# Sums of w1's gradient laid out as they are stored, and a first product with w2 begun earlier, on one Trainium2 core

## The chip, the core and the metric

The kernel runs on one core of one Trainium2 chip. Such a core has an engine for matrix products (TensorE, "PE" in the profile; its weight loads are listed apart as "PEld"), three others that compute (VectorE "DVE", ScalarE "ACT", GpSimd "POOL"), an engine that mostly issues transfers (SyncE "SP"), and 16 DMA engines that carry the transfers of all of them. Products land in PSUM, a small memory of eight banks, and are copied from there to SBUF by ACT or DVE. The metric is the device time of one execution in microseconds (us); lower is better.

## What is computed

The reference runs two kinds of layers, each twice, and differentiates the result with respect to all inputs but one. What is left out here are the set-up, and the convolution `_A_ref` in full.

```python
def _fwd_reference(A_q, A_k, A_v, A_shift_k, A_ssm_k, A_ssm_D, B_x, B_w1, B_w2):
    def _A_ref(q, k, v, shift_k, ssm_k, ssm_D):
        ...
        return q * y
    def _B_ref(x, w1, w2):
        h = jnp.einsum("bsd,df->bsf", x, w1)
        h = _silu(h)
        out = jnp.einsum("bsf,fd->bsd", h, w2)
        return out
    x = A_q
    x = x + _A_ref(_layernorm(x, axis=-1), A_k, A_v, A_shift_k, A_ssm_k, A_ssm_D)
    x = x + _B_ref(_layernorm(x, axis=-1), B_w1, B_w2)
    x = x + _A_ref(_layernorm(x, axis=-1), A_k, A_v, A_shift_k, A_ssm_k, A_ssm_D)
    x = x + _B_ref(_layernorm(x, axis=-1), B_w1, B_w2)
    return x

def reference(...):
    ...
    _out, _vjp = jax.vjp(_f, A_q, A_k, A_v, A_shift_k, A_ssm_k, A_ssm_D, B_w1, B_w2)
    _grads = _vjp(grad_out)
```

There are 2048 tokens, D = 448 channels and F = 1792 hidden features, all in bfloat16. Two results matter below. The gradient of w1 (448 x 1792) is, for each of the two dense layers, the layer's normalised input, transposed, times the gradient at the hidden features; the two layers' parts are added. The gradient at the hidden features begins with the product of the incoming gradient with w2 transposed; for the second dense layer the incoming gradient is `grad_out` itself, so this product needs nothing of the forward pass.

## The kernel before

**Opening.** `_ssm_prefix` computes the convolution once (both layers share its kernel and its k and v) by transforms written as matrix products. Its last loop is the one that matters: `_fft_stage2` makes 14 chunks of a spectrum and hands each to `cons_prod` (L461), which copies it out of PSUM, multiplies it on DVE with the two kernel spectra (`pab`, L471), stores it, and, two chunks behind, issues the inverse transform `_fft_inv_stage2_chunk` (L235, L236), whose result is copied to `B1`. PSUM is one ring of four buffers here (tag "A"). Behind the loop the first four token tiles of `grad_out` (`k.gb0`, "chunk 0") are transposed on PE (L487) and copied by DVE into `k.gT0`, a part of the tile `X` that is not in use yet (L488); the last products (`ps_y`, L496) give `Ysb`.

**Main part.** `Main.run` goes over the tokens in four chunks of 512. The generators `H` (product with w1, then silu and, beside it, a copy for the slope), `O` (product with w2), `G` (the incoming gradient times w2 transposed), `N` (its result times w1 transposed, and the layer norm's backward) and `T`/`T2` (transposes) each yield after a piece of PE's work. A string of letters fixes the order in which they take turns on PE, whose instruction order is written out by hand. `_products` (L504) makes the seven pairs of feature blocks of `H` and `G`; as 448 = 3 x 128 + 64, it puts the 64-row remainders of two blocks beside each other in two half-height tiles of the array. In the table below "G20" is `G` for the second dense layer of chunk 0, "G21" that of chunk 1:

| Where | Order before (L816, L828 to L831, L858) |
|---|---|
| in front of the first `H` | G20: two pairs, three transposes, G20: one pair |
| after the first forward layer | G20: four pairs; then G21: three pairs between transposes |
| chunk 1's stage | O G G O G G O T O T, the four G being G21's last pairs |

`G` copies each pair from PSUM into `ghT` (tag "T", five buffers, seven feature blocks each).

**Weight gradients.** Both weight gradients need all tokens, so the hidden features and their gradients are transposed by DMA and stored per feature block (`store`, L560). `Jobs` then sums them block by block, as filler: other code calls `jobs.run(n)`, and each step is four products. `load` brings a block of 2048 tokens x 128 features (`dstat`, 512 KB); `mms` (L992) has the block as the stationary side and the 448 channels as the moving side, 16 token tiles for each layer, so that the sum in PSUM is 128 features x 448 channels (L995). For w2 that is how the result is stored. For w1 it is the other way round: `fin_w1` (L1102) copies the sum to SBUF, and `flush` (L1108), one job later, turns it with four PE transposes (L1117), copies it again and stores it. Layer 2 has the moving side `n3m`, layer 1 `n1m`. The order of jobs is in `steps` (L1037): w2's blocks 0 to 6, w1's 14 blocks, w2's blocks 7 to 13. PSUM here is two banks "po", one "jb", one "tr" for the jobs and two double banks "mm" for the suffix.

**Suffix.** `_ssm_suffix` does the convolution's backward with products of its own (`ps_tr`, `ps_gkv`, `ps_gK`, and `ps_sk`, which uses tiles 32 columns wide, L1318), and calls `jobs.run` between them; `jobs.run(1000)` at its end issues what is left. POOL's queue carries most of the suffix's loads and the stores of w1's and w2's gradients.

Of the kernel before, what the change touches and what calls it, by code (L numbers as in the profile page):

```python
# [10 lines left out]
FP32 = mybir.dt.float32  # L11
BF16 = mybir.dt.bfloat16
# [285 lines left out]
def _ssm_prefix(k):  # L298
# [4 lines left out]
    with ExitStack() as es:  # L303
# [133 lines left out]
                    next(ln0, None)  # L437
        for _ in ln0:
            pass
        for i in range(7):  # L440
            _swap_halves_dma(k, KB, Ka, 2048 * i, 2048 * (i + 1), nc.gpsimd)
        stage1_kv(*prev)
# [15 lines left out]
            turn(A1f, Zkv, g)  # L458
        hold = []

        def cons_prod(ci, ps):  # L461
            sl = slice(ci * 1024, (ci + 1) * 1024)
            xs = Zf[:, sl]
            _copy(nc, bal.pick(1024), xs, ps[:])
            if ci % 2 == 1:
                st = nc.gpsimd.dma_start(out=k.SPEC_d["KV"][:, (ci - 1) * 1024:(ci + 1) * 1024], in_=Zf[:, (ci - 1) * 1024:(ci + 1) * 1024])
            if ci == 3:
                with tc.issue_after(st.ins):
                    nc.gpsimd.memset(k.w2T[0:64, 3, 0:2 * P], 0.0)
            pab = work.tile([P, 2, 1024], BF16, name="pab", tag="pab", bufs=3)  # L470
            nc.vector.tensor_tensor(out=pab[:], in0=xs.rearrange("p (a c) -> p a c", a=1).to_broadcast([P, 2, 1024]), in1=ZK[:, :, sl], op=ALU.mult)  # L471
            bal.add("dve", 1.22)
            hold.append((pab[:, 0], pab[:, 1], ci))
            if len(hold) > 2:
                pa, pb, cj = hold.pop(0)
                _fft_inv_stage2_chunk(k, pa, pb, False, B1, cj, psum)

        _fft_stage2(k, Zkv, psum, cons_prod)

        k.X = k.wk.tile([P, NT, D], BF16, name="X", tag="WX")  # L480
        k.gT0 = k.X[:].rearrange("p t d -> p (t d)")[:, 11 * D:11 * D + 2048].rearrange("p (b t) -> p b t", b=ND)
        for pa, pb, cj in hold:
            _fft_inv_stage2_chunk(k, pa, pb, False, B1, cj, psum, halves=cj == NCI - 1)
        pt = psum.tile([P, ND, 512], BF16, name="ps_t", tag="A", bufs=4)
        for b, (lo, hi) in enumerate(BLK):
            for tl in range(4):
                nc.tensor.transpose(pt[:, b, tl * P:(tl + 1) * P], k.gb0[:, tl, lo:hi], k.ident[:])  # L487
        nc.vector.tensor_copy(k.gT0, pt[:])  # L488

        B1v = B1.rearrange("p a (c n s) -> p a c n s", c=2, n=16)  # L490
        for i in range(8):
            py = psum.tile([P, 2, 512], FP32, name="ps_y", tag="A", bufs=4)
# [45 lines left out]
class Main:  # L538
# [162 lines left out]
                nc.gpsimd.dma_start(out=_pm(k.outs[0][0])[:, t - 1:t + 1, :], in_=X[:, t - 1:t + 1, :])  # L701
            yield

    def G(self, gT, res, dT=None, dv=()):
        nc, k = self.nc, self.k
        half = lambda h: self.t([P, NF // 2, 512], f"ghT{h}", "T", 5)
        res[:] = [half(0)]
        gh = res
        for fp, ps in _products(nc, lambda: self.banks("ps_g"), self.w2T, gT):
            if fp == 3:  # L710
                res.append(half(1))
            for lo, hi in self.parts(fp):
                hh, o = divmod(2 * fp + lo, 7)
                g = gh[hh][:, o:o + hi - lo, :]
                d = None if dT is None else self.dpart(dT, 2 * fp + lo, 2 * fp + hi)
                if dT is not None and fp in dv:
                    nc.vector.tensor_tensor(out=g, in0=d, in1=ps(lo, hi), op=ALU.mult)
                    continue
                if dT is None and fp in dv:
                    with self.tc.issue_after(k.ln_last.ins):  # L720
                        nc.vector.tensor_copy(g, ps(lo, hi))
                else:
                    nc.scalar.copy(g, ps(lo, hi))  # L723
                if dT is not None:
                    self.g_last = nc.vector.tensor_tensor(out=g, in0=d, in1=g, op=ALU.mult)
            yield
# [57 lines left out]
    def run(self, es):  # L784
# [22 lines left out]
            nc.gpsimd.dma_start(out=_pm(k.Y_d[:]), in_=k.Ysb[:])  # L807
        nT = self.nT()
        gh2 = []
        g20 = self.G(k.gT0, gh2, dv=(2,))  # L810

        def steps(pattern, **gens):
            for ch in pattern:
                next(gens[ch], None)

        steps("GGtttG", G=g20, t=self.T2(self.n0[0][1], nT))  # L816
        gb = gb_load(0)
        weave("H" * 7, H=self.H(0, 0, nT, r, range(14)))
        aT, dT1 = r
# [5 lines left out]

        gh21 = []
        g21 = self.G(gT, gh21)
        steps("GGGG", G=g20)  # L828
        next(g20, None)
        nT = self.nT()  # L830
        steps("tGtGtGt", G=g21, t=self.T2(self.n1[1], nT))  # L831
        r = []
# [4 lines left out]
        for c in range(4):  # L837
# [38 lines left out]
            if c < 3:  # L876
                r = []
                if c == 0:
                    weave("NTNTNHNNHHNNHHNHH", N=n, T=self.T(self.n0[1][1], nT), H=self.H(c + 1, 0, nT, r, (10, 11)))
                else:  # L880
                    weave("NHNNHHNNHHNNHHN", N=n, H=self.H(c + 1, 0, nT, r))
                gb = gb_load(c + 1)
                aT, dT1 = r
                weave("OOOOOOTOTO", O=self.O(c + 1, 0, aT), T=tg)
                self.fwd1(c + 1, [self.chain] * 4)
                g = self.G(gT, gh1, dT0)
                if c:
                    gT = self.nT()
                    self.load_gT(c + 1, gT)
                    weave("G" * 7, G=g)  # L890
                else:
                    weave("G" * 7, G=g)
                self.slope(dT1, self.last_copy)
            else:
                weave("NJNJNJNJNJNJNJN", N=n, J=jg)
                for hh in range(2):
                    self.store(("g", 1), gh2[hh], c, hh)
                weave("J" * 11 + "TJJTJJJJ", T=tg, J=jg)
                weave("GGGJJGGJJGGJJ", G=self.G(gT, gh1, dT0, (1, 3, 5)), J=jg)
# [23 lines left out]
class Jobs:  # L923


    def __init__(self, k, main):
        self.k, self.nc, self.main = k, k.nc, main
        self.pool = main.ch
        self.n_ld = self.n_bank = 0
        self.pend = None  # L930
        self.last_ld = None

    def gen(self):
# [71 lines left out]
    def group(self, fts, keys, movs, fin, tags=None):  # L1005
        ps = {}
        tags = tags or [None] * len(fts)
        for i, ft in enumerate(fts):
            st = self.load(keys[0], ft)
            ps[ft] = self.bank(tags[i])  # L1010
            yield from self.mms(ps[ft], st, movs[0](), 0, NT, True, False)
        if fts == (12, 13):
            self.go2()
        for ft in fts:
            st = self.load(keys[1], ft)
            if fts == (5, 6) and ft == 5:
                self.load_n3()
            yield from self.mms(ps[ft], st, movs[1](), 0, NT, False, True)
            fin(ft, ps[ft])
# [17 lines left out]
    def steps(self):  # L1037
        g2 = lambda: self.k.mov2
        go = lambda: self.go
        keys = (("a", 1), ("a", 0))  # L1040
        yield from self.opening()
        yield from self.group((3,), keys, (go, g2), self.fin_w2, tags=("jb",))
        yield from self.group((4,), keys, (go, g2), self.fin_w2, tags=("tr",))
        yield from self.group((5, 6), keys, (go, g2), self.fin_w2)
        wkeys = (("g", 1), ("g", 0))
        movs = (lambda: self.n3, self.n1)
        for f in range(12):
            yield from self.group((f,), wkeys, movs, self.fin_w1)
        yield from self.group((12, 13), wkeys, movs, self.fin_w1)
        for f in range(7, 13):  # L1050
            yield from self.group((f,), keys[::-1], (g2, self.go2), self.fin_w2)
        yield from self.last_block(keys[::-1], (g2, self.go2))

    def last_block(self, keys, movs):
# [5 lines left out]
        for lo, hi in ((0, 320), (320, D)):  # L1060
# [6 lines left out]
                        yield 1  # L1067
            nc.scalar.copy(o[:, lo:hi], ps[:, lo:hi])
            nc.sync.dma_start(out=k.outs[8][ft * P:(ft + 1) * P, lo:hi], in_=o[:, lo:hi])
        self.flush()  # L1070

    def go2(self):
        k = self.k
# [21 lines left out]
    def fin_w2(self, ft, ps):  # L1095
        nc, k = self.nc, self.k
        o = self.out()
        nc.scalar.copy(o[:], ps[:, :D])
        self.flush()
        (nc.gpsimd if ft < NF - 2 else nc.sync).dma_start(out=k.outs[8][ft * P:(ft + 1) * P, :], in_=o[:])  # L1100

    def fin_w1(self, ft, ps):  # L1102
        o = self.out()
        self.nc.scalar.copy(o[:], ps[:, :D])
        self.flush()
        self.pend = (ft, o)

    def flush(self):  # L1108
        nc, k = self.nc, self.k
        if self.pend is None:  # L1110
            return
        ft, o = self.pend
        self.pend = None
        out7v = k.outs[7].rearrange("(c p) f -> p c f", p=DC)
        pt = k.psum.tile([DC, ND, P], BF16, name="ps_dt", tag="tr", bufs=1)
        for dc in range(ND):
            nc.tensor.transpose(pt[:, dc, :], o[:, dc * DC:(dc + 1) * DC], k.ident[:])  # L1117
        o7 = k.dp3.tile([DC, ND, P], BF16, name="do7", tag="do7", bufs=2)
        nc.scalar.copy(o7[:], pt[:])
        nc.gpsimd.dma_start(out=out7v[:, :, ft * P:(ft + 1) * P], in_=o7[:])  # L1120


class APart:
# [259 lines left out]
```

## Time and profile before

| | us |
|---|---|
| median of three runs | 717.25 |
| the three runs | 716.99, 717.25, 719.49 |
| the profiled execution | 716.31 |
| its span in the profile | 714.5 |

The profile is of one execution. Its granted clock is 0.995 of full on average: 0.76 between 64 and 78 us, full afterwards.

| Stage | us from the span's start |
|---|---|
| opening | 0 to 102 |
| first products with w2, first `H` | 102.7, 109.2 |
| chunk 1's last forward product with w2 and G21's last pairs | 240.6 to 258.8 |
| w1's gradient, first and last product | 531.9 to 662.8 |
| what is left of w2's gradient, alone on PE | from 678 |

In a row of the profile "L995 PE MATMUL ps_d<-n3m,dstat 128\*128 128x448 x224" is: line, engine, operation, output and inputs, rows and columns of the array in use, the size of the moving side, and the number of instructions. A product's row lasts longer than its share of the engine, since products overlap; the distance between starts tells what one costs. In the chain of waits a line is a start, a length and the work that set the end in that stretch.

### The profile page before, as it was taken

To read this page: it belongs to the slowest core of one execution; us is meant where nothing else is said; L and a number is where in the kernel's file an instruction comes from. 1 tells how busy PE (TensorE), PEld (TensorE's weight loads), DVE (VectorE), ACT (ScalarE), POOL (GpSimd) and SP (SyncE) were. 2 spreads that over 40 slices of the span, in tenths; PEclk is the share of its full clock that TensorE was granted. 3 is DMA by queue.
4 is the path that set the end of the run, shared out by engine and by line. 5 is a ranking of instruction groups with operands and counts; after the bars stand their busy time and mean duration, and the time that the engine had idled before them with its cause. 6 is when DMAs were issued, how large, how long until landed. Compare 5 with 4: busy or idle time off the path is not lost.

```text
span 714.5 us, 12786 instructions
## 1 busy us (share of the span) xinstructions
PE 689.3 (96%) x5008; PEld 380.9 (53%) x5008; DVE 486.2 (68%) x1106; ACT 444.2 (62%) x582; POOL 123.3 (17%) x208
## 2 busy tenths in 40 slices
PE   6997899999999999999999999999999999999998
PEld 4886654434444444444444444544566666656655
DVE  4788776758887747877279723934258769869790
ACT  3878877686777868778677685132755555545200
POOL 1034420111011100111001100001212223353130
PEclk9999899999999999999999999999999999999999
DMA  9949998659969999499975999089999897879962
GB/s 303 305 146 234 342 287 255 168 139 270 236 146 235 215 240 242 116 243 231 224 179 133 233 229 365 3 187 249 309 413 357 291 343 245 266 274 377 354 181 95
DMA packets 196237, 172.59 MB, mean 242 GB/s; under 512 B 143090, under 2 KB 174194, under 8 KB 195024
## 3 DMA queue, kind: packets, MB, share of 16 engines
q1 hardware_dynamic: 181280, 115.30, 61.3%
q0 software_dynamic: 13344, 52.54, 20.9%
q10 hardware_dynamic: 1552, 3.94, 1.5%
q8 instruction: 39, 0.64, 0.4%
q14 instruction: 22, 0.18, 0.1%
HBM read 73.25 MB, written 60.10 MB: 187 GB/s over the span
## 4 chain that ended last, share of the span: by engine, by line
PE 62%; issue 8%; DVE 5%; ACT 4%; DMA 3%; POOL 2%; POOLq 0%; DVEq 0%; ACTq 0%
PE ps_d L995 12%; PE ps_n L741 12%; PE ps_h L513 11%; PE ps_g L513 10%; PE ps_o L695 7%; PE ps_d L1030 3%; ACT dT L688 2%; DMA ksf<-KS_d 1%; PE ps_t L580 1%; PE ps_gK L1305 1%; PE ps_tr L1211 1%; POOL rstd L279 1%; PE ps_d L1065 1%; PE ps_s L206 1%; DVE n L287 1%
## 5 line engine op out<-in xcount | busy, mean ns | idle before, releaser
L995 PEld LDWEIGHTS <-dstat 128*128 128x128 bf16 x768 | 72.5, 98 | 61.1
L513 PE MATMUL ps_h<-nT,w1sb 128*128 128x512 bf16 (+1 forms) x448 | 97.4, 380 | 2.6 <-ACT dT L678 1.9
L741 PE MATMUL ps_n<-w1T,ghT 128*128 128x448 bf16 x448 | 92.5, 353 | 0.8 <-DVE ghT L866 0.8
L695 PE MATMUL ps_o<-w2sb,aT 128*128 128x448 bf16 x448 | 88.5, 352 | 0.0
L513 PE MATMUL ps_g<-nT,w2T 128*128 128x512 bf16 (+1 forms) x392 | 82.9, 380 | 0.1
L723 ACT CAST ghT<-ps_g 128x512 bf16<-128x512 f32 (+1 forms) x74 | 54.1, 760 | 41.5 <-PE ps_g L513 41.2
L673 ACT ACTIVATE aT<-ps_h 128x512 bf16<-128x512 f32 (+1 forms) x82 | 60.0, 759 | 29.2 <-PE ps_h L513 27.6
L513 PEld LDWEIGHTS <-w1sb 128*128 128x128 bf16 (+1 forms) x448 | 35.5, 97 | 59.7 <-issue 25.4
L741 PEld LDWEIGHTS <-ghT 128*128 128x128 bf16 x448 | 43.2, 98 | 42.3 <-DVE ghT L866 1.7
L695 PEld LDWEIGHTS <-aT 128*128 128x128 bf16 x448 | 43.5, 98 | 40.1
L513 PEld LDWEIGHTS <-w2T 128*128 128x128 bf16 (+1 forms) x448 | 35.4, 97 | 55.1 <-issue 20.8
L915 DVE SCALAR_TENSOR_TENSOR lb_v<-lb_u,n 128x448 bf16<-128x448 bf16 x48 | 30.0, 624 | 46.8 <-ACT lb_u L745 46.3
L279 POOL TENSOR_TENSOR rstd<-ln_ve,mhalf 128x2 f32<-128x2 f32 (+2 forms) x27 | 23.0, 851 | 198.8 <-DVE ln_ve L277 198.8
L688 ACT ACTIVATE dT<-dT 128x1024 bf16<-128x1024 bf16 (+1 forms) x64 | 55.0, 940 | 0.1
L995 PE MATMUL ps_d<-n1m,dstat 128*128 128x448 bf16 x224 | 48.6, 352 | 0.0
L995 PE MATMUL ps_d<-n3m,dstat 128*128 128x448 bf16 x224 | 48.6, 352 | 0.0
L678 ACT CAST dT<-ps_h 128x1024 bf16<-128x1024 f32 (+1 forms) x50 | 42.8, 872 | 0.0
L745 ACT ACTIVATE lb_u<-ps_n,rstd 128x448 bf16<-128x448 f32 x32 | 20.7, 647 | 34.5 <-PE ps_n L741 26.3
L995 PE MATMUL ps_d<-X,dstat 128*128 128x448 bf16 x160 | 34.2, 353 | 0.0
L995 PE MATMUL ps_d<-go,dstat 128*128 128x448 bf16 x160 | 33.7, 353 | 0.0
L581 ACT COPY nT<-ps_t 128x1024 bf16<-128x1024 bf16 x20 | 20.2, 1008 | 18.7 <-PE ps_t L580 18.7
L866 DVE TENSOR_TENSOR ghT<-dT,ghT 128x512 bf16<-128x512 bf16 (+2 forms) x24 | 18.1, 778 | 19.2 <-ACT ghT L723 17.0
(217 smaller groups left out, 1245.1 us busy)
## 6 DMA issues: line engine op xcount, KB each, us to landing
dstat<-g_d SPq DMA_DIRECT2D x28, 512.0 KB, 5.6
dstat<-a_d SPq DMA_DIRECT2D x23, 512.0 KB, 7.1
a_d<-turned SPq DMA_DIRECT2D x16, 512.0 KB, 4.1
g_d<-turned SPq DMA_DIRECT2D x16, 512.0 KB, 3.9
a_d<-turned SPq DMA_DIRECT2D x16, 384.0 KB, 3.3
g_d<-turned SPq DMA_DIRECT2D x16, 384.0 KB, 3.3
N_d<-n POOLq DMA_DIRECT2D x10, 448.0 KB, 4.6
spec_K<-ZK POOLq DMA_DIRECT2D x7, 512.0 KB, 7.7
```

The costliest lines, as they stand in the source:

```text
L279: k.ln_pow = nc.gpsimd.tensor_tensor(out=r[:, lo:hi], in0=ve[:, 0:n], in1=k.mhalf[:, 0:n], op=ALU.pow)
L513: nc.tensor.matmul(ps(u, u + 1)[:, 0, :], lhsT=wT[h, b, ft * P:(ft + 1) * P], rhs=rhs[h, b, :], start=start, stop=stop)
L673: self.last_silu = nc.scalar.activation(aT[hh][:, o:o + hi - lo, :], ps(lo, hi), ACT.Silu)
L678: nc.scalar.copy(self.dpart(dT, 2 * fp + lo, 2 * fp + hi), ps(lo, hi))
L688: self.nc.scalar.activation(d[:, o:o + n, :], d[:, o:o + n, :], ACT.Derivative_silu)
L695: nc.tensor.matmul(po[:, :D], lhsT=aT[ft // 7][:, ft % 7, tl * P:(tl + 1) * P], rhs=self.w2sb[:, ft, :], start=(ft == 0), stop=(ft == NF - 1))
L723: nc.scalar.copy(g, ps(lo, hi))
L741: nc.tensor.matmul(pn[:, :D], lhsT=gh[ft // 7][:, ft % 7, tl * P:(tl + 1) * P], rhs=self.w1T[:, ft, :], start=(ft == 0), stop=(ft == NF - 1))
L745: nc.scalar.activation(u0[:], pn[:, :D], ACT.Identity, scale=k.rstd[2 * L + 1][:, t:t + 1], accum_out=cp[:, tl, 0:1])
L915: nc.vector.scalar_tensor_tensor(out=v[:], in0=u0, scalar=-1.0 / D, in1=n_t, op0=ALU.mult, op1=ALU.mult, accum_out=cp[:, 1:2])
L995: self.nc.tensor.matmul(ps[:, :D], lhsT=st[:, t, :], rhs=mov[:, t, :], start=(first and t == 0), stop=(last and t == NT - 1))
L1030: nc.tensor.matmul(ps[ft][:, :D], lhsT=get(t), rhs=mov[:, t, :], start=ft not in seen, stop=(last[ft] == i and t == hi - 1))
```

## The change

Two parts of the diff, cut to the core.

**w1's gradient.** `fin_w1` and `flush` are gone; `pair` takes two feature blocks at a time and has the channels as the stationary side and the block as the moving side, so that the sum is channels x features, as it is stored. Channels 0 to 383 are three products of 128 columns per block. The last 64 channels of both blocks go into one bank, block u in partitions 64u to 64u + 63, by two products with 64 stationary columns each. Each block's sums are copied once and stored by two transfers.

```diff
-        for f in range(12):
-            yield from self.group((f,), wkeys, movs, self.fin_w1)
-        yield from self.group((12, 13), wkeys, movs, self.fin_w1)
+        for i in range(NF // 2):
+            yield from self.pair(i, wkeys, movs)
...
+    def pair(self, i, keys, movs):
+        fts = (2 * i, 2 * i + 1)
+        ps = [self.bank(tag) for tag in (("jb", "tr") if i % 2 else ("po", "po"))]
+        for L in range(2):
+            st = [self.load(keys[L], ft) for ft in fts]
+            n = movs[L]()
+            for t in range(NT):
+                last = L == 1 and t == NT - 1
+                for b in range(3):
+                    cols = slice(b * P, (b + 1) * P)
+                    for u in range(2):
+                        nc.tensor.matmul(ps[u][:, cols], lhsT=n[:, t, cols], rhs=st[u][:, t, :], start=(L == 0 and t == 0 and b == 0), stop=(last and b == 2))
+                    if b == 0:
+                        for u in range(2):
+                            nc.tensor.matmul(ps[0][64 * u:64 * u + 64, 384:512], lhsT=n[:, t, 384:D], rhs=st[u][:, t, :], start=False, stop=False)
+                if t % 2:
+                    yield 1
+            if L == 0 and i == NF // 2 - 1:
+                self.go2()
+        out = k.outs[7]
+        for u, ft in enumerate(fts):
+            o = k.dp3.tile([P, 4, P], BF16, name="dout", tag="do7", bufs=2)
...
+            nc.scalar.copy(o[:, 0:m, :], ps[u][:, 0:m * P].rearrange("p (b f) -> p b f", f=P))
+            cols = slice(ft * P, (ft + 1) * P)
+            nc.gpsimd.dma_start(out=out[0:384, cols].rearrange("(b p) f -> p b f", p=P), in_=o[:, 0:3, :])
+            nc.gpsimd.dma_start(out=out[384:D, cols], in_=o0[64 * u:64 * u + 64, 3, :])
```

**Chunk 0's product with w2.** The transposes of `gb0` now stand in front of the opening's last loop, and DVE copies them out in two pieces (into `gb0` itself and into a part of `X`). `g_step` issues one pair of the product and its copy; it is called in chunks 6 and 10 of the loop and once behind it. The results of the first seven blocks go to `k.gh0`, the second half of `X`, in place of a buffer of tag "T". In `Main.run` the remaining four pairs stand in front of the first `H`, G21 takes the place behind the first forward layer, and nothing of it is left for chunk 1's stage. The memset on `w2T` is issued by POOL earlier. `gh0` serves again as the first half of chunk 0's `ghT` in the first dense layer.

```diff
+        k.gh0 = Xf[:, 8 * D:].rearrange("p (a s) -> p a s", s=512)
+        pt = psum.tile([P, ND, 512], BF16, name="ps_t", tag="A", bufs=4)
...
+        nc.vector.tensor_copy(g3, pt[:, 0:3])
+        nc.vector.tensor_copy(g1, pt[:, 3:4])
...
+        def g_step():
+            fp, ps = next(k.g20)
+            _copy(nc, bal.pick(1024), k.gh0[:, 2 * fp:2 * fp + 2, :], ps(0, 2))
...
+            if ci in (6, 10):
+                g_step()
         _fft_stage2(k, Zkv, psum, cons_prod)
+        g_step()
...
-        g20 = self.G(k.gT0, gh2, dv=(2,))
+        g20 = self.G(None, gh2, dv=(5,), first=k.gh0)
...
-        steps("GGtttG", G=g20, t=self.T2(self.n0[0][1], nT))
+        steps("GGtttGG", G=g20, t=self.T2(self.n0[0][1], nT))
...
         g21 = self.G(gT, gh21)
-        steps("GGGG", G=g20)
         next(g20, None)
+        steps("GGGG", G=g21)
```

More of the change, by code (lines that the diff above doesn't have):

```diff
@@ L439, in _ssm_prefix @@
             pass
+        nc.gpsimd.memset(k.w2T[0:64, 3, 0:2 * P], 0.0)
         for i in range(7):
@@ L459, in _ssm_prefix, with __getitem__, banks @@
         hold = []
+        k.X = k.wk.tile([P, NT, D], BF16, name="X", tag="WX")
+        Xf = k.X[:].rearrange("p t d -> p (t d)")
+        k.gh0 = Xf[:, 8 * D:].rearrange("p (a s) -> p a s", s=512)
+        pt = psum.tile([P, ND, 512], BF16, name="ps_t", tag="A", bufs=4)
+        for b, (lo, hi) in enumerate(BLK):
+            for tl in range(4):
+                nc.tensor.transpose(pt[:, b, tl * P:(tl + 1) * P], k.gb0[:, tl, lo:hi], k.ident[:])
+        g3 = k.gb0[:].rearrange("p t d -> p (t d)")[:, 0:1536].rearrange("p (b s) -> p b s", s=512)
+        g1 = Xf[:, 4 * D:4 * D + 512].rearrange("p (b s) -> p b s", s=512)
+        nc.vector.tensor_copy(g3, pt[:, 0:3])
+        nc.vector.tensor_copy(g1, pt[:, 3:4])
+        bal.add("dve", 1.3)
+        class Sets:
+            def __getitem__(self, at):
+                h, b, cols = at
+                return g3[h, b, cols] if b < 3 else g1[h, 0, cols]
+        def banks():
+            ps = psum.tile([P, 2, 512], FP32, name="ps_g", tag="A", bufs=4)
+            return lambda lo, hi: ps[:, lo:hi, :]
+        k.banks = banks
+        k.g20 = _products(nc, lambda: k.banks(), k.w2T, Sets())
+        def g_step():
+            fp, ps = next(k.g20)
+            _copy(nc, bal.pick(1024), k.gh0[:, 2 * fp:2 * fp + 2, :], ps(0, 2))
         def cons_prod(ci, ps):
@@ L465, in cons_prod @@
             if ci % 2 == 1:
[L466 to L469, printed above, removed]
+                nc.gpsimd.dma_start(out=k.SPEC_d["KV"][:, (ci - 1) * 1024:(ci + 1) * 1024], in_=Zf[:, (ci - 1) * 1024:(ci + 1) * 1024])
             pab = work.tile([P, 2, 1024], BF16, name="pab", tag="pab", bufs=3)
@@ L476, in cons_prod @@
                 _fft_inv_stage2_chunk(k, pa, pb, False, B1, cj, psum)
+            if ci in (6, 10):
+                g_step()
         _fft_stage2(k, Zkv, psum, cons_prod)
-        k.X = k.wk.tile([P, NT, D], BF16, name="X", tag="WX")
-        k.gT0 = k.X[:].rearrange("p t d -> p (t d)")[:, 11 * D:11 * D + 2048].rearrange("p (b t) -> p b t", b=ND)
+        g_step()
         for pa, pb, cj in hold:
             _fft_inv_stage2_chunk(k, pa, pb, False, B1, cj, psum, halves=cj == NCI - 1)
[L484 to L488, printed above, removed]
         B1v = B1.rearrange("p a (c n s) -> p a c n s", c=2, n=16)
@@ L702, in O, with G @@
             yield
-    def G(self, gT, res, dT=None, dv=()):
+    def G(self, gT, res, dT=None, dv=(), first=None):
         nc, k = self.nc, self.k
         half = lambda h: self.t([P, NF // 2, 512], f"ghT{h}", "T", 5)
-        res[:] = [half(0)]
+        res[:] = [half(0) if first is None else first]
+        if gT is None:
+            k.banks = lambda: self.banks("ps_g")
+            prods = k.g20
+        else:
+            prods = _products(nc, lambda: self.banks("ps_g"), self.w2T, gT)
         gh = res
-        for fp, ps in _products(nc, lambda: self.banks("ps_g"), self.w2T, gT):
+        for fp, ps in prods:
             if fp == 3:
@@ L885, in run @@
                 self.fwd1(c + 1, [self.chain] * 4)
-                g = self.G(gT, gh1, dT0)
+                g = self.G(gT, gh1, dT0, first=None if c else k.gh0)
                 if c:
@@ L929, in __init__ @@
         self.n_ld = self.n_bank = 0
-        self.pend = None
         self.last_ld = None
@@ L1011, in group @@
             yield from self.mms(ps[ft], st, movs[0](), 0, NT, True, False)
-        if fts == (12, 13):
-            self.go2()
         for ft in fts:
@@ L1069, in last_block @@
             nc.sync.dma_start(out=k.outs[8][ft * P:(ft + 1) * P, lo:hi], in_=o[:, lo:hi])
-        self.flush()
     def go2(self):
@@ L1098, in fin_w2 @@
         nc.scalar.copy(o[:], ps[:, :D])
-        self.flush()
         (nc.gpsimd if ft < NF - 2 else nc.sync).dma_start(out=k.outs[8][ft * P:(ft + 1) * P, :], in_=o[:])
[L1102 to L1108, printed above, removed]
-        nc, k = self.nc, self.k
[L1110 to L1120, printed above, removed]
+    def pair(self, i, keys, movs):
+        nc, k = self.nc, self.k
+        fts = (2 * i, 2 * i + 1)
[19 more added lines that the diff above has]
+            o = k.dp3.tile([P, 4, P], BF16, name="dout", tag="do7", bufs=2)
+            if u == 0:
+                o0 = o
+            m = 4 - u
+            nc.scalar.copy(o[:, 0:m, :], ps[u][:, 0:m * P].rearrange("p (b f) -> p b f", f=P))
+            cols = slice(ft * P, (ft + 1) * P)
+            nc.gpsimd.dma_start(out=out[0:384, cols].rearrange("(b p) f -> p b f", p=P), in_=o[:, 0:3, :])
+            nc.gpsimd.dma_start(out=out[384:D, cols], in_=o0[64 * u:64 * u + 64, 3, :])
```

## The prediction

> **What bounds the kernel now.** I read the page's first two parts first, then TensorE's waits, then the same idle time by stage.
>
> ```profile
> PE 689.3 (96%) x5008; PEld 380.9 (53%) x5008; DVE 486.2 (68%) x1106; ACT 444.2 (62%) x582; POOL 123.3 (17%) x208
> ...
> PE   6997899999999999999999999999999999999998
> ...
> PEclk9999899999999999999999999999999999999999
> ```
>
> TensorE (PE) is the busy engine from the tenth slice on, at the full granted clock. Busy time alone does not prove a bound, so the waits:
>
> ```profile
> PE ps_v L235 <- DVE pab L471: 7.4, 5, 3.6
> PE ps_kt L354 <- DMA ZK<-in_A_ssm_k_dram: 4.9, 1, 4.9
> PE ps_h L513 <- ACT dT L678: 1.9, 4, 0.5
> PE ps_t L780 <- DVE n L287: 1.5, 1, 1.5
> ```
>
> Those are its largest waits (total us, times, longest). They lie in the opening and the first chunk; the windows (length, then busy time of PE) say where idle time is left:
>
> ```profile
> 64.00:78.00 14.00, 10.35 (x101) 7.96 (x99) 8.22 (x9) 11.62 (x13) 6.41 (x14) 0.76 1.04 252
> 78.00:96.00 18.00, 14.21 (x193) 11.16 (x192) 16.11 (x16) 14.89 (x16) 4.88 (x10) 1.00 0.92 350
> ...
> 520.00:590.00 70.00, 69.76 (x637) 46.05 (x636) 50.25 (x111) 37.93 (x42) 16.42 (x29) 1.00 0.92 346
> 590.00:645.00 55.00, 54.92 (x448) 34.20 (x446) 43.55 (x108) 28.54 (x36) 21.38 (x35) 1.00 0.79 269
> ```
>
> From 520 to 645 us PE idles 0.3 of 125 us. The sums of w1's gradient run here (first on n3m at 531.9 us, last on n1m at 662.8 us by those tiles' rows), as filler between other products. So a microsecond added to PE's own work there comes out at the end, and a wait that is removed from another engine there is worth nothing.
>
> **Part 1, w1's gradient: the products.** Removed: 14 blocks x 2 layers x 16 token tiles = 448 products of 448 columns. Added: per pair of blocks, layer and token tile (7 x 2 x 16 = 224 steps) six products of 128 columns on the full array, and two of 64 stationary columns, one for each half of the output partitions. The chain of waits has the price of each kind:
>
> ```profile
> 525.50 0.76 PE ps_d L995 x4
> 526.25 0.89 PE ps_tr L1211 x16
> ...
> 670.10 1.01 PE ps_sk L1318 x64
> 671.11 1.62 PE ps_d L995 x8
> 672.73 0.22 PE ps_dt L1117 x4
> ```
>
> Four old products take 0.76, so 0.189 each, and 448 take 84.7 us. Sixteen 128x128 instructions, each with its own weight load, take 0.89, so 0.0556 each; the unlike gK products (112 stationary columns) have the same 0.89 per sixteen. The Trainium skill (TensorE: Matmul & The Clock Gate, Back-to-back issue gap) gives about 81 ns for a sustained load-and-product pair at 128 columns; by that each step would cost 7 x 0.025 = 0.18 us more and the sum 40 us more (a rival below); the rows here, with a new load each time, have 56.
>
> The two 64-column products read different data, fill different columns of the array and can run side by side; then a step is 7 slots of 0.0556 = 0.389 us, against 2 x 0.189 = 0.378 before. By columns alone the change is nearly free. What it adds is a change of the array's layout: full, two half-width tiles, full again, in every step. No half-width product is in this trace. The nearest is the shift gradient's, in 32-column tiles, on the timeline of PE (start us, us):
>
> ```profile
> 669.56 0.54 PE L995 MATMUL ps_d<-go,dstat 128*128 128x448 bf16 x2
> 670.03 0.24 PE L1318 MATMUL ps_sk<-kx_s,gks 128*32 128x128 bf16 x4
> ...
> 670.66 0.45 PE L1318 MATMUL ps_sk<-kx_s,gks 128*32 128x128 bf16 x18
> 671.04 0.55 PE L995 MATMUL ps_d<-go,dstat 128*128 128x448 bf16 x2
> ```
>
> In: the second old product starts at 669.56 + 0.19 = 669.75 and leaves at 669.94, but the tiles start at 670.03: 0.09 late. Four tiles start together, so side by side is real. Out: sets of four follow each other every 0.0556; five sets from 670.66 end at 670.94, the next full product starts at 671.04: 0.10 late, and the second one 0.01 late (0.55 less a 0.35 row is 0.20, not 0.189). So 0.20 us a visit. A second witness: sixteen G or H products, four of them half-height in two pairs, take 3.23 on the chain; 14 slots of 1.73 / 8 = 0.216 are 3.02, so 0.21. The lengths before and after differ (448, 512 and 128 columns) and the price does not. The Trainium skill (TensorEngine Tiling (Array Packing), Key Properties) says that changing the tiling mode, not merely the tile, drains TensorE; that speaks against this change, since it would hold for half-width tiles too, which no row here shows. Bounds: 0 (half-width tiles pass without a drain) to 0.23 (the chain's own account of the 32-column visit, 1.01 - 0.89 + 1.62 - 1.51). I take 0.20, the closest row in kind (column tiles).
>
> A step: 0.389 + 0.20 = 0.589; 224 steps 132.0 us. Less 84.7: **+47.3**.
>
> **Part 1, the rest.** The 56 transposes go: 14 x 0.22 = **-3.1** on PE. Gone from ACT is one of two copies per block; ACT is idle 32 of 70 us in 520:590, so 0, and were ACT the bound it would be a gain. POOL issues 28 stores instead of 14 (0.53 us each, the issue rows of POOL), 7.4 us in some 125 us where POOL is busy 38: 0; without that slack the loads of q_g, q_n, q_y behind them would come later by as much, and after them DVE, never PE at once. Loads of dstat now come two per step pair of 9.4 us (16 x 0.589) instead of one per 3.0, landing in 5.6: easier. go2 is loaded behind the last pair's first half, 9.4 + 3 us before its use, landing 10.2: 0. The last pair holds both "po" banks and block 7 of w2's gradient takes one of them, so PE waits once for a copy like L1098's or L723's (0.6 to 0.76): **+0.6** (0 to 1).
>
> **Part 2, chunk 0's product with w2.** Work on PE is the same; it moves. Three of seven pairs (24 products) go into the opening, four in front of H where three were, chunk 1's seven pairs take the place behind the first forward layer, and the second chunk's stage loses its four:
>
> ```profile
> 247.22 3.40 PE L513 MATMUL ps_g<-nT,w2T 128*128 128x512 bf16 x16
> 250.45 1.49 PE L695 MATMUL ps_o<-w2sb,aT 128*128 128x448 bf16 x7
> 252.00 3.39 PE L513 MATMUL ps_g<-nT,w2T 128*128 128x512 bf16 x16
> ```
>
> - Those leave: 2 x 3.23 = -6.5. What they hid is late next: ACT's slope runs to 251.0, and the backward product needs DVE to multiply by it. PE would arrive at 252.1; I leave 0.4 for the transposes' copies behind the slope: **-6.1** (-6.5 to -4).
> - In front of H: 24 products (4.95 us with one layout visit) become 32 (6.45), +1.5; H waits 0.7 for nT now (108.29 to 109.22 less one slot), which the last two pairs cover: **+0.8** (0.5 to 1.7).
> - In the opening: 24 products, 4.95 us, put among products that wait for DVE. PE idles 3.8 us in 78:96, so about **+1.2**. Bounds: +4.95 if none fits (DVE is busy 16.1 and ACT 14.9 of 18 us there and carry three more copies of 1.0 to 1.2), and -2.8 if the transposes put in front shorten the pause at 66 to 70 us and the half clock after it (0.76 in 64:78; 5.5 us of products at 106 ns) goes. The two copies out of those transposes, 1.25 us, stand on DVE where it idles 2.16 before its first product at 68.97. The memset on w2T moves past three stores of ks on POOL; its load was issued at 29.5 and the slot is at 33 to 36: 0, up to 1 us if it lands late, as conv waits for those stores' buffers.
>
> Sum of part 2: -4.1.
>
> **Sum.** 47.3 - 3.1 + 0.6 - 4.1 = +40.7 on the profiled execution's span of 714.5 us: 755.2; with the 1.8 us around it (716.31) 757.0. The median of the runs is 0.9 above that run: **758 us**.
>
> **Rivals.**
> - No drain for half-width tiles (the faster side). Then the 224 visits cost nothing and part 1 is 2.6 - 3.1: 758 - 44.8 = 713. For it: no 128*64 row exists. Against: both layouts that do exist, row and column, pay on every visit. It decides where the visit costs under 0.02 us. Chance 0.07.
> - Only one of the two changes drains: 758 - 22.4 = 736. Against: 0.09 and 0.10 on either side. 0.05.
> - The two halves run one after the other, though drained: 224 x 0.0556 = 12.5 more: 770. Against: four tiles start within 0.01 us above. 0.04.
> - Weight loads no longer hide (a load's row is 98 ns): between 56 and 98 ns a product, 7 x 0.042 x 224 = 66 more at most: 824. By the skill's 81 ns, 798. Against: ps_tr and gK. 0.02.
> - Part 2 does not do what it says: every gap it fills was free and chunk 1 stalls for the slope: 762, inside the forecast's range.
>
> **Chances.** Forecast 0.82. One per cent of the time is 7 us, and half of that about what a measurement can tell from no change. All cases but the first rival are far slower; that one lies at the edge (0.6% faster): faster 0.05, same 0.02, slower 0.93. The range: 734 takes in the one-sided drain, 770 the serial halves and the opening's worst; the forecast's own is 748 to 766.
>
> **What would show it.** In the profile after: 0.09 to 0.10 us between a full product and the half-width pair on either side, in every step; the pair starting together; 0.0556 between full products; PE still without idle time by semaphore from 430 us; about 47 us between the first and last w1 product more than before; the second chunk's stage 6 us shorter. Wrong if steps take 0.39 (no drain) or over 0.65, or if PE waits for dstat, a bank or DVE in that stretch.

## The result

The changed kernel takes 760.9 us (median of four runs, 760.12 to 762.23) against 717.12 of the kernel before (four runs, 712.58 to 719.49): a ratio of 1.062, 95% interval 1.0566 to 1.0675. The profiled execution took 760.12 us with a span of 758.3, against 716.31 and 714.5. The kernel before took a median of 715.66 and 715.44 us in the 34 later runs beside the experiments, so the change costs nearer to 45 us than to 44. In the two spans, stage by stage:

| Stage, by the starts of PE's products | before, us | after, us | difference | forecast |
|---|---|---|---|---|
| up to the start of the opening's last transposes of a spectrum | 58.89 | 55.45 | -3.44 | 0 |
| from there to the first `H` (opening's loop, G20) | 50.33 | 51.72 | +1.4 | +2.0 |
| to the suffix's first product (all four chunks) | 393.34 | 386.89 | -6.45 | -6.1 |
| suffix with w1's gradient, to the end | 211.94 | 264.24 | +52.3 | +44.8 |
| span | 714.5 | 758.3 | +43.8 | +40.7 |

The profile after, the first part of its page and PE's longest waits (total us, times, longest):

```profile
PE 733.0 (97%) x6251; PEld 431.6 (57%) x6296; DVE 488.4 (64%) x1108; ACT 436.0 (57%) x566; POOL 131.0 (17%) x222
```
```profile
PE ps_kt L354 <- DMA ZK<-in_A_ssm_k_dram: 4.2, 1, 4.2
PE ps_v L235 <- DVE pab L499: 3.8, 3, 2.7
PE ps_h L535 <- ACT dT L700: 1.9, 4, 0.5
PE ps_t L808 <- DVE n L287: 1.5, 1, 1.5
```

PE has gained 44 us of "busy" time, nearly all that the span has gained, and its waits for other engines have become fewer (ps_v on pab 3.8 where it was 7.4). Read alone that would say that PE does more work. It does not: the columns that it streams are the same when a pair of half-width products, which runs side by side, is counted once (7 x 128 = 2 x 448 in a step). A row of a busy share does not tell a product from the pause before the next one; the starts do. Two steps of w1's sums, from PE's timeline of the kernel after (start us, us from first start to last end):

```profile
560.00 0.25 PE L1141 MATMUL ps_d<-dstat,n3m 128*64 128x128 bf16 x2
560.18 0.51 PE L1138 MATMUL ps_d<-dstat,n3m 128*128 128x128 bf16 x6
560.62 0.25 PE L1141 MATMUL ps_d<-dstat,n3m 128*64 128x128 bf16 x2
560.80 0.40 PE L1138 MATMUL ps_d<-dstat,n3m 128*128 128x128 bf16 x4
```

A step is 560.62 - 560.00 = 0.62 us (by the rows' exact starts 0.618, and between 0.616 and 0.620 in each of the 166 steps that nothing else interrupts). Six full products after 560.18 would be through at 560.18 + 6 x 0.0557 + 0.01 = 560.52; the half-width pair starts at 560.62, 0.09 late by the exact starts. The pair itself starts together and would be through at 560.06; the next full product starts at 560.18, 0.12 late. Seven slots of 0.0557 are 0.39; the other 0.227 us of a step are the two changes of layout, 224 times.

And the second chunk's stage, where G21's last pairs are gone, from PE's timelines of the kernel before (first fence) and after:

```profile
257.00 1.49 PE L695 MATMUL ps_o<-w2sb,aT 128*128 128x448 bf16 x7
258.33 0.61 PE L580 MATMUL ps_t<-ident,n 128*128 128x128 bf16 x8
258.77 1.49 PE L741 MATMUL ps_n<-w1T,ghT 128*128 128x448 bf16 x7
```
```profile
248.54 1.49 PE L717 MATMUL ps_o<-w2sb,aT 128*128 128x448 bf16 x7
249.87 0.61 PE L602 MATMUL ps_t<-ident,n 128*128 128x128 bf16 x8
250.31 1.49 PE L769 MATMUL ps_n<-w1T,ghT 128*128 128x448 bf16 x7
```

The backward product starts 8.46 us earlier; 2.07 of these were there at the first backward product of chunk 0 already (168.81 and 166.74), so 6.4 came in between, where G21's last pairs had stood. Nothing stands between the transposes and the product: the wait for ACT's slope that was feared here is not there.

### The profile page after: what moved, and what is told of

The parts are those of the page before. It is cut to its first block, busy times and chain, and to the rows that moved or that the text cites. A ratio compares the mean times of both kernels' runs of the same rounds, so it can differ in the third digit from the quotient of the medians.

```text
span 758.3 us, 15319 instructions
## 1 busy us (share of the span) xinstructions
PE 733.0 (97%) x6251; PEld 431.6 (57%) x6296; DVE 488.4 (64%) x1108; ACT 436.0 (57%) x566; POOL 131.0 (17%) x222
## 4 chain that ended last, share of the span: by engine, by line
PE 84%; ACT 5%; DVE 4%; issue 4%; POOL 1%; DMA 1%; SPq 0%; POOLq 0%
PE ps_d L1138 13%; PE ps_n L769 11%; PE ps_g L535 10%; PE ps_h L535 9%; PE ps_d L1022 8%; PE ps_o L717 7%; PE ps_d L1141 5%; PE ps_v L235 3%; PE ps_d L1055 2%; PE ps_v L236 2%; PE ps_cv L392 2%; PE ps_tr L370 1%; PE ps_t L602 1%; PE ps_s L206 1%; ACT A1K L111 1%
## 5 line engine op out<-in xcount | busy, mean ns | idle before, releaser
L769 PE MATMUL ps_n<-w1T,ghT 128*128 128x448 bf16 x392 | 81.4, 353 | 0.8 <-DVE ghT L894 0.8
L535 PE MATMUL ps_g<-nT,w2T 128*128 128x512 bf16 (+1 forms) x378 | 81.0, 380 | 1.1 <-issue 0.5
L751 ACT CAST ghT<-ps_g 128x512 bf16<-128x512 f32 (+1 forms) x65 | 47.2, 752 | 36.8 <-PE ps_g L535 36.4
L1138 PE MATMUL ps_d<-dstat,n3m 128*128 128x128 bf16 x672 | 62.7, 221 | 0.3
L1138 PE MATMUL ps_d<-dstat,n1m 128*128 128x128 bf16 x672 | 62.0, 221 | 0.1
L769 PEld LDWEIGHTS <-ghT 128*128 128x128 bf16 x392 | 37.9, 98 | 37.3 <-DVE ghT L894 1.7
L1022 PEld LDWEIGHTS <-dstat 128*128 128x128 bf16 x320 | 30.7, 98 | 29.6 <-issue 2.1
L1138 PEld LDWEIGHTS <-n3m 128*128 128x128 bf16 x672 | 39.8, 98 | 10.6
L1138 PEld LDWEIGHTS <-n1m 128*128 128x128 bf16 x672 | 39.4, 98 | 9.2
L111 ACT CAST B1v<-ps_v 128x1024 bf16<-128x1024 f32 x14 | 14.2, 1012 | 45.5 <-PE ps_v L236 45.5
```

What stands on the lines that cost most here:

```text
L535: nc.tensor.matmul(ps(u, u + 1)[:, 0, :], lhsT=wT[h, b, ft * P:(ft + 1) * P], rhs=rhs[h, b, :], start=start, stop=stop)
L769: nc.tensor.matmul(pn[:, :D], lhsT=gh[ft // 7][:, ft % 7, tl * P:(tl + 1) * P], rhs=self.w1T[:, ft, :], start=(ft == 0), stop=(ft == NF - 1))
L1022: self.nc.tensor.matmul(ps[:, :D], lhsT=st[:, t, :], rhs=mov[:, t, :], start=(first and t == 0), stop=(last and t == NT - 1))
L1138: nc.tensor.matmul(ps[u][:, cols], lhsT=n[:, t, cols], rhs=st[u][:, t, :], start=(L == 0 and t == 0 and b == 0), stop=(last and b == 2))
```

## The experiments

The kernel before was run beside each group; its medians were 715.66 us (11 runs, beside the first four kernels) and 715.44 (23 runs, beside the last four).

**The second part alone.** Edit: the changed kernel with the job class of the kernel before.

```diff
-        for i in range(NF // 2):
-            yield from self.pair(i, wkeys, movs)
+        for f in range(12):
+            yield from self.group((f,), wkeys, movs, self.fin_w1)
+        yield from self.group((12, 13), wkeys, movs, self.fin_w1)
```

> Only the second part of the change: chunk 0's product with w2 begun in the opening; w1's gradient as before. Theory (the parts are independent, the second gains by moving products into idle time): about 712 us, the before's 717 less 4 to 6; chunk 1's stage 6.4 us shorter, the opening 1.4 us longer. Rival (the gain seen in the profiled execution is run-to-run variation of the first loads): no difference from before beyond 0.3%.

Measured: 711.44 us (710.57 to 712.29), ratio 0.9938, interval 0.992 to 0.9957. So the second part gains 4.2 us, and it is the fastest kernel here. The gain is no accident of one execution's first loads: its slowest run is below the fastest of the 11 beside it (713.57). In its profile the stretch from the last transposes to `H` takes 52.04 us (50.33 before), and from `H` to the end of the forward products 326.7 (333.0).

**The first part alone.** Edit: the kernel before with the job class of the changed kernel.

```diff
-        for f in range(12):
-            yield from self.group((f,), wkeys, movs, self.fin_w1)
-        yield from self.group((12, 13), wkeys, movs, self.fin_w1)
+        for i in range(NF // 2):
+            yield from self.pair(i, wkeys, movs)
```

> Only the first part: w1's gradient as it is stored; the opening as before. Theory: 717 plus 52, about 769 us, with steps of 0.617 us in w1's sums as in the changed kernel. Rival (the opening's new order makes the suffix wait somehow): less than 765.

Measured: 764.54 us, ratio 1.0689, interval 1.0656 to 1.0723: 48.9 more than before. The steps are the same 0.618 us. It is 4 us short of the first expectation and just inside the rival's bound. The 52 was the growth of the suffix in one pair of profiles. By that measure this kernel grows by 51.1 (263.0 against 211.9), but its opening, which the edit does not touch, is 2.5 us shorter in this execution than in the profile before. The rival's mechanism is not needed: 48.9 less the 4.2 of the second part is 44.7, and both together, run earlier, are 45.2 above the same median (43.8 above that of the runs beside them), so the parts add up within 1 us. A wait of 1 to 2 us of the rival's kind is not ruled out. The suffix takes 213.9 us in the second part alone, where PE waits 0.9 us for loads of `dstat` and 0.8 at `ps_gkv`, two waits that the profile before does not have; the kernel with quarter-width tiles below has the new opening too, and neither wait.

**Full array in place of half-width tiles.** Edit:

```diff
-                            nc.tensor.matmul(ps[0][64 * u:64 * u + 64, 384:512], lhsT=n[:, t, 384:D], rhs=st[u][:, t, :], start=False, stop=False)
+                            nc.tensor.matmul(ps[u][:, 384:512], lhsT=n[:, t, 320:D], rhs=st[u][:, t, :], start=False, stop=False)
...
-            nc.gpsimd.dma_start(out=out[384:D, cols], in_=o0[64 * u:64 * u + 64, 3, :])
+            nc.gpsimd.dma_start(out=out[384:D, cols], in_=o[64:128, 3, :])
```

> The changed kernel, with the last 64 channels taken by a full-array product per block: 128 stationary columns, channels 320 to 447, of which the upper half is stored. Eight full products a step and no change of layout. Theory (each change of layout costs about 0.23 us a visit): steps of 8 x 0.0557 = 0.445 us, 224 x 0.172 = 38.5 us less than the changed kernel, about 722 us. Rival (the many short products with their weight loads cost it, whatever the layout): the eighth slot adds, 761 us or more.

Measured: 723.85 us, ratio 1.0124, interval 1.0092 to 1.0156. More columns are streamed than in the changed kernel, in as many instructions, and 37 us are gone. Its chain of waits (start us, length):

```profile
560.18 0.11 PE ps_d L1141 x2
560.29 0.34 PE ps_d L1138 x6
560.63 0.11 PE ps_d L1141 x2
```

A step is 0.45 us, eight slots of 0.0557, with nothing lost around the products of line 1141, which are full-width here. The rival (many short products are dear) is out.

**Four quarter-width tiles in place of two half-width.** Edit:

```diff
-                            nc.tensor.matmul(ps[0][64 * u:64 * u + 64, 384:512], lhsT=n[:, t, 384:D], rhs=st[u][:, t, :], start=False, stop=False)
+                            for v in range(2):
+                                q = 64 * u + 32 * v
+                                nc.tensor.matmul(ps[0][q:q + 32, 384:512], lhsT=n[:, t, 384 + 32 * v:416 + 32 * v], rhs=st[u][:, t, :], start=False, stop=False)
```

> The changed kernel, with each 64-column product split into two of 32 columns: four tiles side by side instead of two, the same sums in the same places, the same number of layout changes. Theory A (the exit of 0.12 instead of 0.10 us comes from the wider weight load of a 64-column tile): steps about 0.59 us, 224 x 0.024 = 5 us less, about 755 us. Theory B (the exit costs 0.12 whenever 128-column products follow): 761 us or slightly more.

Measured: 761.53 us, ratio 1.0655, interval 1.062 to 1.0689: the time of theory B. The rows say that neither is quite right. Duration of a tile's product (ns, min/median/max) in the kernel after, in this one, and of the shift gradient's tiles in the kernel before:

```profile
L1141 PE MATMUL ps_d<-dstat,n3m x224: 243/243/244, 523.6 to 691.3; 128*64 128x128 bf16 x112
```
```profile
L1143 PE MATMUL ps_d<-dstat,n3m x448: 229/230/230, 527.3 to 693.6; 128*32 128x128 bf16 x150
```
```profile
L1318 PE MATMUL ps_sk<-kx_s,gks x224: 219/219/230, 666.5 to 677.9; 128*32 128x128 bf16 x112
```

The first tiles after a change of layout take 11 ns longer at 32 columns and 24 at 64, later ones do not (the shift gradient's visits have 15 further sets behind the first; for 64 columns see the sixteen-tile kernel below). The narrower tiles save 14 ns at the exit (0.162 instead of 0.176 us from the last tile's start to the next full product), but four starts are spread over 0.010 us instead of 0.003: a step is 0.611 instead of 0.618 us, 0.007 less where theory A has 0.024. That is 1.5 us in all, lost among what else differs from run to run.

**Two token tiles per visit.** Edit: the half-width products of two tiles stand together, behind block 1 of the second.

```diff
-                    if b == 0:
-                        for u in range(2):
-                            nc.tensor.matmul(ps[0][64 * u:64 * u + 64, 384:512], lhsT=n[:, t, 384:D], rhs=st[u][:, t, :], start=False, stop=False)
+                    if b == 2 and t % 2 == 1:
+                        for tt in range(t - 1, t + 1):
+                            for u in range(2):
+                                nc.tensor.matmul(ps[0][64 * u:64 * u + 64, 384:512], lhsT=n[:, tt, 384:D], rhs=st[u][:, tt, :], start=False, stop=False)
```

> The changed kernel, with the half-width products of two token tiles put together: 112 changes of layout and back instead of 224, the same products. Theory (each visit costs 0.227 us, the products are cheap): 112 x 0.227 = 25.4 us less than the changed kernel, about 735 us. Rival (the 64-column products themselves are slow, wherever they stand): the same as the changed kernel, 761.

Measured: 737.17 us, ratio 1.0287, interval 1.0249 to 1.0326: 23.7 us less than the changed kernel for 112 visits less, 0.21 a visit. The same products in the same number take half the penalty; the products are not slow. A visit on PE's timeline:

```profile
559.86 0.30 PE L1139 MATMUL ps_d<-dstat,n3m 128*64 128x128 bf16 x4
560.09 0.29 PE L1141 MATMUL ps_d<-dstat,n3m 128*128 128x128 bf16 x2
```

Four products last 0.30 from the first start to the last end. The second pair's rows are 0.219 long, so it starts 0.08 behind the first, not 0.056, and the full product follows 0.235 behind the visit's start: two slots and 0.12. By these rows a visit of two pairs costs 0.227 us, as a visit of one did. The 1.7 us by which the time misses the theory are matched by waits of 1.8 us for loads of `dstat` in this profile, which the changed kernel's does not have.

**All sixteen token tiles per visit.** Edit: as above, with 16 in place of 2.

```diff
-                    if b == 2 and t % 2 == 1:
-                        for tt in range(t - 1, t + 1):
+                    if b == 2 and t % 16 == 15:
+                        for tt in range(t - 15, t + 1):
```

> The changed kernel, with the half-width products of all 16 token tiles of a layer put together: 14 visits instead of 224. Theory: 210 x 0.227 = 47.7 us less, about 713 us, if a pair of half-width products in a row costs one slot of 0.0557. Rival (their weight loads, 106 ns by their rows against 98, do not hide when they follow each other): each pair costs up to 0.106, 210 x 0.05 = 10.6 us more than that, about 724. Against the kernel with the second part alone (711.4) it says whether the new layout of w1's sums can be had for nothing: the theory has it 2 us behind.

Measured: 715.55 us, ratio 0.9988, interval 0.9967 to 1.0009: no change against the kernel before, and 4 us behind the second part alone. On PE's timeline a visit is

```profile
533.61 1.08 PE L1139 MATMUL ps_d<-dstat,n3m 128*64 128x128 bf16 x32
534.63 0.29 PE L1141 MATMUL ps_d<-dstat,n3m 128*128 128x128 bf16 x2
```

Sixteen pairs from 533.61; the next full product starts at 534.63, and 16 x 0.0557 + 0.12 is 1.01. So a pair of half-width products does cost one full slot when another stands before it, and their weight loads (110 ns by their rows) hide. The rival's price is out. The longer first pair is there once in each visit:

```profile
L1139 PE MATMUL ps_d<-dstat,n3m x224: 219/219/243, 533.6 to 651.3; 128*64 128x128 bf16 x112
```

By the exact starts the second pair stands 0.080 behind the first, the later ones 0.056 apart, and the next full product is 0.096 late behind the last pair instead of 0.120. The 0.024 is paid between the first pair and the second instead of at the exit, and the visit still costs 0.227 us. Of the 2 us that the time is above the theory, 1.7 are a wait that the next experiment explains.

**No half-width products.** Edit; the gradient of w1's last 64 channels is left out but for the first token tile of each pair.

```diff
-                    if b == 0:
+                    if b == 0 and t == 0 and L == 0:
```

> The changed kernel with the 64-column products left out but for the first token tile of each pair: the gradient of w1's last 64 channels is not computed. Theory (a step is six full products of 0.0557 and a visit of 0.283): 217 x 0.283 = 61.4 us less than the changed kernel, about 699 us. Rival (the full products are slowed too, by their number of weight loads): less is saved.

Measured: 719.16 us, one run: 20 more than the theory, and more than the sixteen-tile kernel that does all of the work. The full products are not slowed (0.056 from start to start). PE waits:

```profile
PE ps_gkv L1320 <- ACT gkv L1322: 7.8, 1, 7.8
...
PE ps_v L235 <- DVE pa L1276: 4.7, 1, 4.7
```

These two waits are not in the kernel after. What lies behind the first is on this kernel's chain of waits (start us, length):

```profile
619.29 8.22 DMA q_y<-Y_d
...
632.35 1.00 DVE skx L1307
...
634.48 1.16 POOL kx_s L1295
635.63 6.46 DMA gks<-in_A_v_dram
...
642.85 0.92 ACT gkv L1322
643.81 1.65 PE ps_gkv L1320 x4
```

So the suffix has a second chain, through POOL's queue: loads for q's gradient, DVE's work on them, and only then, behind a store and a memset on POOL, the load of v for the next products. It is nearly as long as PE's. Take enough work from PE and this chain sets the time; the pauses also bring the half clock back (two stretches of 6.8 us in this execution). In the sixteen-tile kernel the same product waits 1.7 us. That is why work added to PE here comes out one for one and work removed does not, as far as one execution shows it.

**The second part without the opening's three pairs.** Edit, on the second part alone:

```diff
-            if ci in (6, 10):
-                g_step()
...
-        g_step()
...
-        steps("GGtttGG", G=g20, t=self.T2(self.n0[0][1], nT))
+        steps("GGGGtttGGG", G=g20, t=self.T2(self.n0[0][1], nT))
```

> The second part alone (w1's gradient as before), but no pair of chunk 0's product with w2 in the opening's loop: all seven stand in front of the first forward product. Theory (the opening's three pairs cost 1.9 us there and 4.95 us elsewhere): 3 us more than the second part alone, about 714.5 us, and 1 to 2 us less than before. Rival (the opening had no idle time to give): as the second part alone, 711.4.

Measured: 714.8 us, ratio 0.9993, interval 0.9973 to 1.0013: 3.4 us behind the second part alone. The windows of the stretch from the last transposes to `H` (length, then busy time of PE), here and in the second part alone:

```profile
57.93:113.34 55.41, 47.24 (x486) 31.13 (x484) 38.55 (x51) 43.84 (x54) 15.86 (x29) 0.97 1.05 311
```
```profile
55.85:107.89 52.04, 45.30 (x485) 30.45 (x484) 39.77 (x52) 42.67 (x50) 15.92 (x29) 1.00 1.00 285
```

The same products take 3.4 us less when three pairs stand in the loop's pauses. This kernel is 0.6 us below the kernel before, which the interval does not tell from nothing, where 1 to 2 were expected. Nearly all of the second part's gain depends on these three pairs: moving G21's pairs out of the second chunk's stage only pays because the place that they take over has been emptied into idle time.

## Why the prediction was right

- **The bound.** PE sets the pace from 520 us on, and work added to it came out at the end: the steps' 0.618 us instead of 0.378 make 53.8 us in 224 steps, less 3.1 for the transposes, and the suffix grew by 52.3.
- **The mechanism.** The drain on both sides of the half-width pair, which no row of the kernel before showed for this layout, is there, and taking it away (full array, 37 us; sixteen tiles per visit, 45 us) takes the loss away. The Trainium skill (TensorEngine Tiling (Array Packing), Key Properties) says that a change of the tiling mode drains TensorE; the rows agree, 0.09 us on the way in and 0.12 on the way out.
- **The size: the term that was mis-sized.** "So 0.20 us a visit" measured 0.227: 0.093 in, 0.120 out, 0.003 between the two starts, 0.010 on the second full product. The forecast read only the two ends of the shift gradient's visit. Counted over its whole length, the same lines give more: 16 sets from 670.03 would be through at 670.03 + 16 x 0.0557 = 670.92, and the next full product starts at 671.04, 0.12 late and not 0.10. What the last five sets do not show is that the second set starts 0.065 behind the first instead of 0.056, and that the four starts of a set are spread over 0.010. The whole visit costs 0.22 there, close to the bound of 0.23 that the forecast named and did not take. One set or many makes no difference: 0.227 with one, two or sixteen pairs of 64 columns, 0.220 with one set of four tiles of 32. 224 x 0.027 = 6 us of the 7.5 us by which the suffix was short. The rest is the wait for the bank behind the last pair, 0.8 by the starts instead of 0.6, and a pause of 1.3 us inside w2's block 7, which the first part alone does not have; what it waited for was not found.
- **The price of a full product.** 0.0556 forecast, 0.0558 on average in the 664 distances between the full products of the uninterrupted steps. The Trainium skill's 81 ns for such a pair (TensorE: Matmul & The Clock Gate, Back-to-back issue gap) would have made 40 us more by estimate (224 x 7 x 0.025); the rows do not agree with it.
- **The second part.** -6.4 where -6.1 stood, +1.4 where +2.0 stood. Seven profiles with the new opening give 51.2 to 52.0 us for the stretch up to `H`, the two with the old one 50.3 and 49.4, so +1.9 is the better figure. The possible 2.8 us from a shorter half clock did not come: the half-clock stretch shrank from 6.8 to 3.4 us in the kernel after and was absent in the second part alone, and the stretch took as long with either.
- **What was not forecast.** The -3.4 us before the opening's last transposes is not the change's. In the profiles of this case that point lies anywhere from 55.5 to 59.3 us, the new opening at both ends of that, the old at 57.3 and 58.9. The two profiles part before 23 us. PE's first product, behind the wait for a load, starts at 4.87 in the one and 4.24 in the other. And the products of `ps_s` at L206, 448 columns each, start 0.373 us apart until 17.8 us in the profile before, twice the 0.188 of later ones, but 0.188 apart from their first at 11.7 us in the profile after; this makes 1.7 of the 3.4. Two single profiles should not be compared across that stretch.
- **Luck.** This stretch hid almost half of the 7.5 us by which the suffix was short, so the difference of the two spans (+43.8 for +40.7) looks better than its largest term. By the medians the change cost about 45 us, 4 to 5 more than forecast.
- **The rivals.** No drain: out by the rows. One-sided drain: out, both sides pay. Serial halves: out, the starts are 0.003 us apart. Weight loads in the open: out, full products still start 0.056 apart. Part 2 not doing what it says: out, by itself it gains 4.2 us.

## What to carry to other kernels

Count the changes of TensorE's tile layout, not only its columns: here one visit to half-width tiles and back cost four times the product slot for which it was made, and half-width products went at full speed only when many stood together (even then the kernel was 4 us behind the old layout of w1's sums). Price such a visit from the product in front of it to the second one behind it, over its whole length; its two ends alone gave 0.20 where the whole gives 0.22. Before an engine's time is cut, find out how far behind the next chain is; here it was a few microseconds, and the one kernel that cut deeper was no faster.

## What the hardware showed unexpectedly

The first product after a change of layout lasts longer by its row: 230 ns at 32 columns and 243 at 64, against 219 for later ones, and 229 to 232 for the first full one on the way back. The excess is paid once in each visit, as a later start of the second set or, where there is no second set, of the full product behind. The Trainium skill (TensorE: Matmul & The Clock Gate, LDWEIGHTS) puts a weight load at its columns divided by 1.2 GHz, by estimate 27 ns more for 64 columns than for 32; the products' rows have 13 more, and the rows of the loads themselves 14 (106 ns and 92). That the load is what is seen was not tested by itself.
